# A longer annealed task order, and the last output rows in halves of columns, in an attention and gated-convolution kernel

## The chip, the cores and the metric

The kernel runs on one core of a Trainium2 chip. A core has a matrix engine (TensorE, "PE" in the profile; its weight loads are listed as "PEld"), a vector engine (VectorE, DVE), a scalar engine (ScalarE, ACT), a general engine (GpSimd, POOL) and a sync engine (SyncE, SP). The engines run side by side, each through its own list of instructions in order, and wait for each other through semaphores. Data come from device memory by DMA, issued here from the queues of SP (loads) and ACT (stores). The metric is the device time of one execution in microseconds.

## The reference

Inputs are queries, keys and values of 8 batches, 8 heads, 512 local and 32 global tokens, head size 64. A global token attends to all 544 tokens. A local token attends to the 32 global ones and to the local ones at a distance of at most 32. The attended rows (8 x 544 x 512) go through a gated block:

```
k_all, v_all = concat(global, local)
out_g = softmax(q_g k_all^T / 8) v_all
out_l = softmax(concat(q_l k_g^T, masked q_l k_l^T) / 8) v_all
x     = concat(out_g, out_l), heads side by side       # 8 x 544 x 512
gate  = sigmoid(sum over k of conv_w[k] * x shifted by k)   # 5 taps, causal
out   = (gate * (x @ w_val)) @ w_out                   # 512 x 512 weights
```

The weights come in float64, everything else in float32.

## The kernel before

**Units and batches.** The work is cut into 32 units, each two heads of one batch, so that one unit is 128 of the 512 columns of x for one batch; four units make a batch. The matmuls of the gated block are done in three passes of split operands (high times high, low times high, high times low), which stands for one float32 product.

**Tasks.** The kernel first adds some 1,400 named tasks to a `Plan`, each with an engine, a cost in ns, the tasks it depends on, and buffers it takes and gives. `ORDER` is one string, written out by hand, that names them in the order in which they are emitted. `Plan.order` walks it; every engine gets its own tasks in that order. Nothing is reordered later, so where a task's input is late, its engine stands with everything behind it. The costs of the plan set no order; they only decide how many idle matmuls `keep_clock` puts into expected gaps at the start.

**The names.** For unit u and head h:

- `s`u (PE, L478) scores into one PSUM tile per head (`sx`, `sy`); `mx`u.h (DVE, L490) mask and row minimum; `exp`u.h (ACT, L497); `t`u.h (PE, L503) transposes; `tc`u.h (ACT, L506) copies them to `pts`; `av`u (PE, L514) weighted values; `norm`u (DVE, L521 to L524) divides by the row sum; `xt`u (PE, L533) transposes; `xc`u (ACT, L537) copies.
- `halo`, `tap`, `conv`u.0 to .3 (DVE, L544 to L572): the five taps of the gate, one instruction each. For units 0 to 2 the taps are matmuls `pc`u.k (PE, L597) with diagonal weights that `dg`u (ACT, L586) builds. `sig`u (ACT, L605) is the sigmoid. `xh`u (ACT, L565) and `xl`u (DVE, L568) split x.
- For batch b: `gs`, `gmax`, `gexp`, `gt`, `gtc`, `gav`, `gnorm`, `gx`, `gxc` do the same for the global tokens.
- `g1.`b.e.t (PE, L621): first product, output block e, inner block t, three matmuls of 512 columns; `gv.`b.e (DVE, L629) multiplies by the gate; `gh.`b.e (ACT, L632) and `gl.`b.e (DVE, L635) split the result; `g2.`b.r.e (PE, L643): second product for 128 rows r; `ob.`b.r (ACT, L649) copies it out of PSUM; `st.`b.r (ACT's queue, L814) stores it. The PSUM tiles of g1 and g2 are two (`mm`), so a third waits until gv or ob has read the first.
- `w`k.s0 to .s7 (DVE, L282 to L294) turn a float64 weight block into two float32 parts, `w`k.high (ACT, L352) rounds the high part; k = 0 to 3 is w_val, 4 to 7 w_out.
- `iq`, `iv`, `wi` (SP, L314) issue the loads of a unit's queries and keys, of its values, and of a weight block. Each is made to wait for the PE task that precedes it in `ORDER`.

**Buffers.** One score tile per head (so `s`u+1 waits for `mx`u), two PSUM tiles for transposes, one for `av`, two for g1, g2 and `pc`; in SBUF four qk and four v tiles.

**The end.** Behind batch 7 come the 256 rows of all global tokens as a batch of their own, key `g`: `gxh`, `gxl`, `gconv` (DVE) build its x and gate, `sigg` its sigmoids, then g1, gv, gh, gl of 256 columns, and two g2 blocks of 128 rows. `ob.g.1` is the last copy: ACT takes columns 0 to 255 (L649), DVE columns 256 to 511 (L651). `st.g.r` stores four batches' rows by four DMAs of 32 rows, in turn from SP's and ACT's queues (L836).

**Table loads.** ACT loads another function table whenever it goes from exp to sigmoid or back (ACT_TABLE_LOAD in the profile).

Of the kernel before, what the change touches and what calls it, by code (L numbers as in the profile page):

```python
# [8 lines left out]
F32 = mybir.dt.float32  # L9
# [41 lines left out]
cw s0 mx0.0 mx0.1 w0.s0 exp0.1 exp0.0 w0.s1 w0.s2 s1 t0.1 mx1.0 t0.0 w0.s3 mx1.1 exp1.0 w0.s4 w0.s5 w0.s6 w0.high  # L51
tc0.1 tc0.0 av0 dg0 s2 exp1.1 norm0 mx2.0 xt0 xc0 w1.s0 t1.1 halo0 pc0.0 tc1.1 w1.s1 w1.s2 mx2.1 w1.s3 w0.s7 xh0 t1.0
w1.s4 exp2.1 tc1.0 exp2.0 pc0.1 w1.s5 pc0.2 xl0 av1 w1.s6 w1.high s3 norm1 mx3.0 dg1 exp3.0 t2.1 mx3.1 tc2.1 xt1 wi4
t2.0 w3.s0 w3.s1 w3.s2 pc0.3 tc2.0 t3.0 w3.s3 pc0.4 tc3.0 w1.s7 gs0 iq4 w3.s4 xc1 halo1 exp3.1 av2 w3.s5 w3.high
gmax0.0 wi5 pc1.0 gmax0.1 gexp0.0 iq5 norm2 w4.s0 xh1 pc1.1 w3.s6 w4.s1 w4.s2 gexp0.1 t3.1 xt2 w4.s3 tc3.1 w3.s7
conv0.3 gt0.0 s4 xc2 av3 pc1.2 w4.s4 gtc0.0 mx4.0 w4.high mx4.1 w4.s5 iq6 w5.s0 exp4.0 exp4.1 w4.s6 w5.s1 iq7 t4.0
w4.s7 w5.s2 gav0.0 tc4.0 gnorm0.0 t4.1 w5.s3 dg2 s5 tc4.1 w5.high gt0.1 pc1.3 w5.s4 gtc0.1 mx5.0 w2.s0 w5.s5 gav0.1
exp5.0 mx5.1 w5.s6 pc1.4 gnorm0.1 norm3 iv4 t5.0 exp5.1 w5.s7 tc5.0 t5.1 w2.s1 xl1 gx0 xt3 tc5.1 gxc0 gs1 wi6 halo2
iv5 xh2 fix0 iv6 conv1.3 gmax1.0 w2.s2 pc2.0 xc3 tap3 pc2.1 gmax1.1 fix1 w2.s3 pc2.2 gexp1.0 av4 xh3 pc2.3 pc2.4 norm4
iv7 w6.s0 halo3 w2.s4 xl2 gexp1.1 s6 w6.s1 w2.s5 gt1.0 conv2.3 wi7 w6.s2 xl3 mx6.0 gtc1.0 mx6.1 conv3.0 xt4 w6.s3  # L60
g1.0.0.0 g1.0.0.1 g1.0.0.2 w2.s6 w2.high w6.s4 conv3.1 exp6.0 g1.0.0.3 w6.s5 g1.0.1.0 g1.0.1.1 conv3.2 t6.0 g1.0.1.2
xc4 gav1.0 w6.s6 iq8 w6.high exp6.1 tc6.0 conv3.3 gnorm1.0 av5 g1.0.1.3 w6.s7 sig0 gt1.1 w2.s7 norm5 s7 gv.0.0 sig1
xt5 w7.s0 g1.0.2.0 gh.0.0 w7.s1 gtc1.1 gv.0.1 sig2 xh4 g1.0.2.1 sig3 mx7.0 tap4 g1.0.2.2 w7.s2 iq9 xc5 w7.s3 t6.1
g1.0.2.3 tc6.1 iq10 gl.0.0 g1.0.3.0 g1.0.3.1 av6 gav1.1 mx7.1 s8 gh.0.1 w7.s4 xl4 iq11 exp7.0 t7.0 gv.0.2 gl.0.1 w7.s5
g1.0.3.2 gnorm1.1 g1.0.3.3 iv9 gh.0.2 mx8.0 gl.0.2 iv8 exp7.1 gv.0.3 g2.0.0.0 gx1 exp8.0 g2.0.0.1 tc7.0 w7.s6 iv10
w7.s7 gh.0.3 gxc1 w7.high gl.0.3 mx8.1 g2.0.0.2 norm6 t7.1 exp8.1 t8.0 halo4 tc7.1 g2.0.0.3 g2.0.1.0 xh5 g2.0.1.1 t8.1
conv4.0 conv4.1 conv4.2 ob.0.0 halo5 g2.0.1.2 tc8.0 g2.0.1.3 tc8.1 conv4.3 xt6 xl5 gs2 tap5 xc6 gmax2.0 av7 xh6
conv5.0 g2.0.2.0 gmax2.1 norm7 conv5.1 g2.0.2.1 tap6 iv11 g2.0.2.2 ob.0.1 gexp2.0 gexp2.1 xl6 g2.0.2.3 conv5.2 xt7
gt2.0 conv5.3 s9 g2.0.3.0 halo6 st.0.0 g2.0.3.1 mx9.0 gtc2.0 conv6.0 xc7 g2.0.3.2 iq12 xh7 av8 mx9.1 gav2.0 iq13
exp9.0 exp9.1 s10 g2.0.3.3 xl7 ob.0.2 t9.0 norm8 gnorm2.0 conv6.1 st.0.2 st.0.1 conv6.2 tc9.0 t9.1 conv6.3 tc9.1 xt8  # L70
mx10.0 halo7 xc8 g1.1.0.0 gt2.1 gtc2.1 av9 mx10.1 tap7 gav2.1 exp10.1 conv7.0 g1.1.0.1 ob.0.3 conv7.1 g1.1.0.2
g1.1.0.3 s11 conv7.2 gnorm2.1 conv7.3 exp10.0 sig4 xh8 sig5 gx2 norm9 tap8 iv13 g1.1.1.0 t10.1 sig6 xl8 iq14 xt9 iv14
gv.1.0 g1.1.1.1 g1.1.1.2 gxc2 t10.0 halo8 tc10.1 gh.1.0 conv8.0 mx11.0 iq15 xc9 gl.1.0 g1.1.1.3 g1.1.2.0 sig7 halo9
g1.1.2.1 mx11.1 tap9 tc10.0 av10 st.0.3 g1.1.2.2 exp11.0 g1.1.2.3 conv8.1 s12 gv.1.1 gh.1.1 g1.1.3.0 conv8.2 gv.1.2
exp11.1 mx12.0 t11.0 g1.1.3.1 gh.1.2 exp12.0 t11.1 g1.1.3.2 iv12 gl.1.1 mx12.1 tc11.1 tc11.0 g1.1.3.3 norm10 gl.1.2
xh9 xl9 xt10 conv8.3 conv9.0 exp12.1 gv.1.3 g2.1.0.0 conv9.1 g2.1.0.1 t12.1 xc10 tc12.1 t12.0 tc12.0 av11 gh.1.3 gs3
g2.1.0.2 norm11 xt11 gl.1.3 xh10 gmax3.0 gmax3.1 g2.1.0.3 conv9.2 gexp3.0 g2.1.1.0 halo10 ob.1.0 gexp3.1 conv9.3
g2.1.1.1 tap10 xc11 g2.1.1.2 g2.1.1.3 ob.1.1 s13 iq16 xl10 xh11 av12 st.1.1 gt3.0 st.1.0 halo11 mx13.0 g2.1.2.0
conv10.0 mx13.1 g2.1.2.1 norm12 iv15 s14 exp13.0 exp13.1 conv10.1 conv10.2 mx14.0 conv10.3 xl11 iq17 gtc3.0 exp14.0
xt12 g2.1.2.2 t13.0 xc12 tap11 t13.1 g2.1.2.3 conv11.0 tc13.0 tap12 mx14.1 ob.1.2 tc13.1 g2.1.3.0 g2.1.3.1 av13  # L80
# [164 lines left out]
def attention_moe(ctx, tc, qk, vw, maskd, w_val, convT, w_out, out):  # L245
# [62 lines left out]
    def on_pe(ins):  # L308
        last_pe[:] = [ins.ins]
# [301 lines left out]
    def moe(key, n, x0, deps_x, deps_gate, before, store):  # L611
# [34 lines left out]
        def ob(r):  # L646
# [3 lines left out]
            if at < DM:  # L650
                V.tensor_copy(box["ob", r][:, at:], box["po", r][:, at:])  # L651
# [279 lines left out]
```

## Time and profile before

| | us |
|---|---|
| median of 3 runs | 372.37 |
| lowest, highest | 372.1, 372.75 |
| profiled execution, its own time | 372.69 |
| its span, first to last instruction | 370.9 |
| PE busy | 358.4 |
| DVE busy | 312.0 |
| ACT busy | 257.2 |
| mean granted TensorE clock | 0.999 |

The 1.8 us between the span and the profiled execution's own time lie around the instructions. A row of the page's groups reads: line, engine, operation, output <- inputs, shape, count | busy time, mean ns of one | idle time of the engine just before them and what ended it. A row of the timeline reads: start, duration, engine, line, operation. PE's matmuls are pipelined and overlap in the list, so the step from one start to the next says what one costs, and a busy PE isn't yet PE at its peak. In the last 40 us, DVE and ACT have little left to do, while PE runs through g1 and g2 of batch 7 and of the global tokens.

### The profile page before, as it was taken

The numbers are of one execution on the slowest core, as the hardware profiler recorded it, in microseconds if no ns is written. First come the engines' busy times: TensorE is split into PE (matmuls) and PEld (weight loads), VectorE is DVE, ScalarE is ACT, GpSimd is POOL, SyncE is SP. The second block draws the span as 40 slices with busy tenths as digits, with TensorE's granted clock in tenths as the row PEclk, the third lists the DMA queues.
The fourth block names the chain that finished last, engine by engine and source line by source line (L and its number), as shares of the span: only waits on it lengthen the run. The fifth ranks groups of instructions, "written<-read, shape, count | busy, mean of one in ns | idle before, by whom it ended". The sixth has DMA issues, their size and how long they took to land.

```text
span 370.9 us, 14811 instructions
## 1 busy us (share of the span) xinstructions
PE 358.4 (97%) x6347; PEld 280.5 (76%) x6347; DVE 312.0 (84%) x1094; ACT 257.2 (69%) x620; POOL 0.9 (0%) x7
## 2 busy tenths in 40 slices
PE   7899899999999999999999999999999999999995
PEld 3556557877878787787877887788788888888894
DVE  4899999999998897998689968999768877684861
ACT  3898867976798676976886668977876568434231
POOL 0000000000000000000000000000000000000000
PEclk9999999999999999999999999999999999999999
DMA  8995686495667174881339361975853010011112
GB/s 288 398 340 199 212 302 229 158 357 177 198 218 269 49 267 111 304 310 78 129 120 358 128 195 74 323 220 188 268 214 110 4 58 30 30 57 59 55 61 57
DMA packets 17250, 66.74 MB, mean 180 GB/s; under 512 B 1952, under 2 KB 4000, under 8 KB 17184
## 3 DMA queue, kind: packets, MB, share of 16 engines
q1 hardware_dynamic: 12240, 57.12, 44.4%
q10 hardware_dynamic: 4944, 8.67, 6.4%
q8 instruction: 50, 0.82, 0.9%
q14 instruction: 16, 0.13, 0.1%
HBM read 56.87 MB, written 8.91 MB: 177 GB/s over the span
## 4 chain that ended last, share of the span: by engine, by line
PE 81%; DVE 9%; DMA 7%; issue 1%; ACT 1%; ACTq 0%
PE po L643 23%; PE pv L621 23%; PE ax L514 8%; PE pt L503 6%; PE sx L478 5%; PE ax L533 3%; DMA wraw<-in_w_val_dram 3%; DMA v<-in_vw_dram 2%; PE sy L478 2%; PE ag L446 2%; DVE pm L490 2%; PE pvg L621 2%; PE pog L643 1%; PE gs_sx L403 1%; PE gpt L426 1%; PE pc L597 1%
## 5 line engine op out<-in xcount | busy, mean ns | idle before, releaser
L497 ACT ACTIVATE pm<-pm,mx 128x128 f32<-128x128 f32 x256 | 80.8, 394 | 13.9 <-DVE mx L490 13.4
L572 DVE SCALAR_TENSOR_TENSOR gate<-xc,cw,gate 128x512 f32<-128x512 f32 x116 | 86.1, 748 | 1.4
L643 PE MATMUL po<-woh,gh 128*128 128x512 f32 x128 | 54.2, 424 | 0.5 <-issue 0.5
L621 PE MATMUL pv<-xh,wvh 128*128 128x512 f32 x128 | 54.5, 426 | 0.0
L621 PE MATMUL pv<-xl,wvh 128*128 128x512 f32 x128 | 50.4, 394 | 0.0
L643 PE MATMUL po<-woh,gl 128*128 128x512 f32 x128 | 50.3, 393 | 0.0
L621 PE MATMUL pv<-xh,wvl 128*128 128x512 f32 x128 | 50.2, 392 | 0.0
L643 PE MATMUL po<-wol,gh 128*128 128x512 f32 x128 | 50.1, 391 | 0.0
L506 ACT COPY pts<-pt 128x512 f32<-128x512 f32 x64 | 36.6, 587 | 15.8 <-PE pt L503 15.3
L514 PEld LDWEIGHTS ax<-v,pts 128*32 128x32 f32 x2048 | 30.6, 109 | 11.2 <-issue 3.7
L503 PE MATMUL pt<-ident,pm 128*128 128x128 f32 x256 | 37.3, 274 | 1.3 <-DVE mx L521 0.6
L478 PE MATMUL sx<-qk 64*32 64x128 f32 x1024 | 38.0, 274 | 0.3 <-DVE mx L490 0.3
L503 PEld LDWEIGHTS pt<-ident,pm 128*128 128x128 f32 x256 | 30.5, 140 | 10.2 <-ACT pm L497 1.9
L478 PE MATMUL sy<-qk 64*32 64x128 f32 x1024 | 36.8, 274 | 0.5 <-DVE mx L490 0.4
L514 PE MATMUL ax<-v,pts 128*32 128x65 f32 x2048 | 35.7, 221 | 1.5 <-ACT pts L506 1.4
L478 PEld LDWEIGHTS sx<-qk 64*32 64x32 f32 x1024 | 28.7, 105 | 8.4 <-issue 3.6
L490 DVE CUSTOM_DVE_ANT_0 pm<-sx,mask 128x128 f32<-128x128 f32 x128 | 29.4, 286 | 4.1 <-PE sx L478 4.1
L632 ACT CAST gh<-gv 128x512 fp32r<-128x512 f32 x32 | 19.6, 622 | 18.2 <-DVE gv L629 15.9
L649 ACT COPY ob<-po 128x512 f32<-128x512 f32 x32 | 18.7, 584 | 18.5 <-PE po L643 18.4
L629 DVE TENSOR_TENSOR gv<-pv,gate 128x512 f32<-128x512 f32 x32 | 22.0, 687 | 10.8 <-PE pv L621 10.7
L537 ACT COPY xc<-ax 128x512 f32<-128x512 f32 x32 | 18.9, 589 | 15.4 <-DVE gate L572 12.9
L490 DVE CUSTOM_DVE_ANT_0 pm<-sy,mask 128x128 f32<-128x128 f32 x128 | 29.4, 286 | 0.0
(114 smaller groups left out, 653.4 us busy)
## 6 DMA issues: line engine op xcount, KB each, us to landing
v<-in_vw_dram SPq DMA_DIRECT2D x32, 975.0 KB, 6.7
qk<-in_qk_dram SPq DMA_DIRECT2D x32, 624.0 KB, 4.3
out_dram<-ob ACTq DMA_DIRECT2D x32, 256.0 KB, 2.4
wraw<-in_w_val_dram SPq DMA_DIRECT2D x4, 512.0 KB, 12.3
wraw<-in_w_out_dram SPq DMA_DIRECT2D x4, 512.0 KB, 4.6
mask<-in_mask_dram SPq DMA_DIRECT2D x1, 256.0 KB, 4.4
out_dram<-obg SPq DMA_DIRECT2D x4, 64.0 KB, 1.7
out_dram<-obg ACTq DMA_DIRECT2D x4, 64.0 KB, 2.0
```

Of the source, the lines that this page charges most:

```text
L478: on_pe(T.matmul((sx, sy)[h][32 * j:32 * j + 32, i, :], qkt[rows, 32 * m:32 * m + 32], qkt[rows, k0:k0 + P], start=True, stop=True))
L490: V.tensor_tensor_reduce(out=pm[:, h, i, :], in0=s[:, i, :], in1=mask[:, i, :], op0=ALU.add, op1=ALU.min, scale=-SCALE, scalar=3.0e38, acc ...
L497: A.activation(out=pm[:, h, i, :], in_=pm[:, h, i, :], func=AF.Exp, bias=mx[:, c:c + 1], scale=-1.0)
L503: on_pe(T.transpose(pt[:, i, :], pm[:, h, i, :], ident))
L506: A.copy(st[u]["pts"][:, h], st[u]["pt", h])
L514: on_pe(T.matmul(ax[32 * j:32 * j + 32, h, E1 * i:E1 * i + E1], pts[:, h, i, 32 * j:32 * j + 32], vt[:, block_win(4 * i + j), h, :], start ...
L537: A.copy(xc[:, KW - 1:], flat(u)[:, SL:])
L572: V.scalar_tensor_tensor(out=acc, in0=xc[:, k:k + SL], scalar=cw[:, u % NDT, k:k + 1], in1=acc, op0=ALU.mult, op1=ALU.add)
L621: on_pe(T.matmul(box["pv", e], w[:, e, t * P:t * P + P], x, start=(t == 0 and q == 0), stop=(t == NDT - 1 and q == 2)))
L629: V.tensor_tensor(out=box["gv", e], in0=box["pv", e], in1=gates[x0 + e], op=ALU.mult)
L632: A.copy(box["gh"][:, e, :], box["gv", e])
L643: on_pe(T.matmul(box["po", r], g[:, e, rs], w[:, e, :], start=(e == 0 and q == 0), stop=(e == NDT - 1 and q == 2)))
```

## The change

Two things change.

1. `ORDER` is replaced by another order of the same 1,435 tasks, with one new task, `half`. Dependencies, buffers and all instructions of those tasks but the last rows' are untouched. Its beginning, two stretches of its middle and its end, with the old ones:

```diff
-cw s0 mx0.0 mx0.1 w0.s0 exp0.1 exp0.0 w0.s1 w0.s2 s1 t0.1 mx1.0 t0.0 w0.s3 mx1.1 exp1.0 w0.s4 w0.s5 w0.s6 w0.high
-tc0.1 tc0.0 av0 dg0 s2 exp1.1 norm0 mx2.0 xt0 xc0 w1.s0 t1.1 halo0 pc0.0 tc1.1 w1.s1 w1.s2 mx2.1 w1.s3 w0.s7 xh0 t1.0
...
-xc4 gav1.0 w6.s6 iq8 w6.high exp6.1 tc6.0 conv3.3 gnorm1.0 av5 g1.0.1.3 w6.s7 sig0 gt1.1 w2.s7 norm5 s7 gv.0.0 sig1
-xt5 w7.s0 g1.0.2.0 gh.0.0 w7.s1 gtc1.1 gv.0.1 sig2 xh4 g1.0.2.1 sig3 mx7.0 tap4 g1.0.2.2 w7.s2 iq9 xc5 w7.s3 t6.1
...
-gl.g.2 gl.g.3 g2.g.0.1 g2.g.0.2 g2.g.0.3 g2.g.1.0 ob.g.0 g2.g.1.1 st.g.0 g2.g.1.2 g2.g.1.3 ob.g.1 st.g.1
+cw s0 dg0 mx0.0 mx0.1 w0.s0 exp0.0 w0.s1 exp0.1 w0.s2 s1 dg1 t0.1 tc0.1 t0.0 w0.s3 tc0.0 w0.s4 w0.s5 w0.s6 dg2 mx1.0
+mx1.1 av0 norm0 s2 exp1.1 mx2.0 exp1.0 xt0 w1.s0 xc0 halo0 w1.s1 exp2.0 w1.s2 mx2.1 t1.1 pc0.0 t1.0 tc1.1 xh0 tc1.0
...
+w5.s7 gav1.0 wi7 xh4 av5 w6.s3 gv.0.0 tc6.0 g1.0.2.0 gv.0.1 w6.s4 g1.0.2.1 norm5 sig2 gnorm1.0 mx6.1 sig3 w6.s5
+g1.0.2.2 g1.0.2.3 w7.s0 iq9 gh.0.0 xt5 w6.s6 gl.0.0 gh.0.1 gt1.1 w6.high g1.0.3.0 w7.s1 gl.0.1 g1.0.3.1 w7.s2 xc5
...
+gmax7.0 g1.5.0.1 conv25.0 g1.5.0.2 g1.5.0.3 gexp7.0 conv24.3 g1.5.1.0 g1.5.1.1 gmax7.1 xt26 g1.5.1.2 g1.5.1.3 gv.5.0
+gexp7.1 s28 xc26 av27 g1.5.2.0 g1.5.2.1 mx28.0 tap26 sig21 halo26 iv30 gt7.0 sig22 gh.5.0 conv25.1 exp28.0 iv29
...
+g2.g.0.3 st.7.2 g2.g.1.0 ob.g.0 st.g.0 g2.g.1.1 half g2.g.1.2 g2.g.1.3 ob.g.1 st.g.1
```

2. The last 128 rows (`g2.g.1`, `ob.g.1`, `st.g.1`). Its four PE tasks keep their names, but the first two now make columns 0 to 255 over all four inner blocks, the other two columns 256 to 511: 24 matmuls of 256 columns where there were 12 of 512. After the second, `half` copies the first 256 columns (ACT) and stores them from ACT's queue. `ob.g.1` then copies columns 256 to 383 on ACT and 384 to 511 on DVE, and each quarter is stored by one DMA, from ACT's and SP's queue. The stores of the global rows become one DMA for all four batches of a block, so `st.g.0` is one DMA from ACT's queue where it was four from two queues.

```diff
+            cols, es = slice(0, DM), [e]
+            if (key, r) == END:
+                cols, es = slice(e // 2 * HALF, e // 2 * HALF + HALF), [e % 2 * 2, e % 2 * 2 + 1]
+            for e in es:
+                for q, (g, w) in enumerate(((box["gh"], woh), (box["gh"], wol), (box["gl"], woh))):
+                    on_pe(T.matmul(box["po", r][:, cols], g[:, e, rs], w[:, e, cols], start=(e == 0 and q == 0),
+                             stop=(e == NDT - 1 and q == 2)))
...
         def ob(r):
+            if (key, r) != END:
+                box["ob", r] = sb.tile([P, DM], F32, tag="ob", name=f"ob{key}_{r}")
+                A.copy(box["ob", r], box["po", r])
+                return
+            at = HALF + HALF // 2
+            A.copy(box["ob", r][:, HALF:at], box["po", r][:, HALF:at])
+            V.tensor_copy(box["ob", r][:, at:], box["po", r][:, at:])
+
+        def first_half(r):
+
             box["ob", r] = sb.tile([P, DM], F32, tag="ob", name=f"ob{key}_{r}")
-            at = DM // 2 if (key, r) == ("g", n // P - 1) else DM
-            A.copy(box["ob", r][:, :at], box["po", r][:, :at])
-            if at < DM:
-                V.tensor_copy(box["ob", r][:, at:], box["po", r][:, at:])
+            A.copy(box["ob", r][:, :HALF], box["po", r][:, :HALF])
+            store(r, box["ob", r], ((A, 0, HALF),))
...
-    def store_g(r, o):
-        for s in range(P // SG):
-            (A if s % 2 else nc.sync).dma_start(out[r * (P // SG) + s, 0:SG, :], o[s * SG:s * SG + SG, :])
+    def store_g(r, o, parts):
+        n = P // SG
+        for queue, a, z in parts:
+            queue.dma_start(out[r * n:r * n + n, 0:SG, a:z], o[:, a:z])
```

`HALF` is 256, `END` is the block ("g", 1), and `parts` lists queue, first and last column of each store.

More of the change, by code (lines that the diff above doesn't have):

```diff
@@ L56 @@
[L56 to L60, printed above, removed]
@@ L66 @@
[L66 to L70, printed above, removed]
@@ L71 @@
[L71 to L80, printed above, removed]
```

155 lines of the change are left out of this document (88 added, 67 removed).

## The prediction

> **What bounds the kernel now.** I read the head of the page first, then a table by stage, then single rows where the stage is decided.
>
> ```profile
> PE 358.4 (97%) x6347; PEld 280.5 (76%) x6347; DVE 312.0 (84%) x1094; ACT 257.2 (69%) x620; POOL 0.9 (0%) x7
> 28.00:80.00 52.00, 49.22 (x995) 35.63 (x985) 50.78 (x191) 41.87 (x106) 0.00 (x0) 1.00 0.67 231
> 80.00:115.00 35.00, 34.57 (x749) 27.47 (x748) 32.92 (x115) 27.39 (x66) 0.00 (x0) 1.00 0.68 240
> 180.00:320.00 140.00, 139.58 (x2613) 112.44 (x2603) 115.51 (x414) 104.04 (x246) 0.00 (x0) 1.00 0.47 160
> ```
>
> The windows give the stretch, its length, then the busy time of PE, PEld, DVE and ACT. Over the whole span PE is the long line. From 28 to 80 us another engine sets the pace: DVE is busy 50.78 of 52.00 us and PE 49.22. From 180 to 320 us PE is busy 139.58 of 140 us, while DVE has 24 us to spare and ACT 36. So time can be won in three ways: PE gets more done for the same DVE work early, PE loses fewer waits later, or the tail behind the last matmul shrinks. An order moves work but removes none.
>
> **The early stage, counted.** The new order runs the same tasks, so I compared the sets of tasks ahead of two places. In the old order, 66 PE tasks and 99 DVE tasks stand up to the point where `g1.0.2.0` follows `gv.0.0`, which frees its bank. In the new order the next place that DVE decides is `g2.0.0.2`, which needs `gl.0.2`. Up to there it has the same 66 and 99 tasks, without exception, and 14 PE tasks and 16 DVE tasks more. The 16 are gv.0.1 to 0.3, gl.0.0 to 0.2, mx7.0, mx7.1 and the eight steps of w7.
>
> ```profile
> 57.89 0.69 DVE L286 SCALAR_TENSOR_TENSOR wa<-wraw,wa 128x512 int32<-128x512 int32 x1
> 58.50 0.42 DVE L288 TENSOR_SCALAR wraw<-wa 128x512 int32<-128x512 int32 x1
> 58.83 0.42 DVE L293 TENSOR_SCALAR wraw<-wraw 128x512 int32<-128x512 int32 x1
> ...
> 64.92 0.68 DVE L629 TENSOR_TENSOR gv<-pv,gate 128x512 f32<-128x512 f32 x1
> 65.52 0.42 DVE L282 TENSOR_SCALAR wa<-wraw 128x512 int32<-128x512 int32 x1
> ...
> 66.91 0.28 DVE L490 CUSTOM_DVE_ANT_0 pm<-sx,mask 128x128 f32<-128x128 f32 x1
> ...
> 67.75 0.48 DVE L560 TENSOR_SCALAR gate<-xc,cw 128x512 f32<-128x512 f32 x1
> ```
>
> These timeline rows are DVE without a gap, so the step from one start to the next is the price of a task: gv 0.60 (64.92 to 65.52), two-input weight step 0.61 (57.89 to 58.50), one-input step 0.33 (58.50 to 58.83), mx 0.84 (66.91 to 67.75). A weight is three steps of the first kind and five of the second, 3.5 us (I take 3.6); I price gl like gv, same form. Sum: 6 x 0.60 + 2 x 0.84 + 3.6 = 8.9 us. DVE left gv.0.0 at 65.52, so it leaves gl.0.2 at 74.4. With about 0.15 us for the end of the instruction and the hand-over, PE can start `g2.0.0.2` at **74.55**.
>
> ```profile
> 73.37 0.66 PE L503 MATMUL pt<-ident,pm 128*128 128x128 f32 x4
> 73.78 0.48 PE L621 MATMUL pv<-xh,wvh 128*128 128x512 f32 x1
> ...
> 76.75 0.40 PE L643 MATMUL po<-woh,gh 128*128 128x512 f32 x1
> ```
>
> In the old order the row at 76.75 is the same `g2.0.0.2`. By then PE has done the same tasks and two more, t7.0 (73.37 to 73.78, 0.41 us) and the single matmul of gx1. Same content: 76.3. **The new order is ahead by 76.3 - 74.55 = 1.75 us.** The condition is that the common 99 tasks still end at 65.5. Bounds: between 28 and 80 us DVE idles 1.2 us. If that went, the gain would be near 3; if it came twice, near 0.5. I take it unchanged, since buffers and first loads are the same and two moves work against each other there: dg0 and dg1 now stand ahead of exp0 and tc0 on ACT (about 1.5 us each), while w0.high and exp1.0 step back behind them.
>
> SP's order moves too, and here it costs.
>
> ```profile
> 54.49 0.33 SPq L314 DMA_DIRECT2D wraw<-in_w_out_dram  x1
> 62.09 0.15 DVE L452 TENSOR_SCALAR gd<-ag 128x1 f32<-128x1 f32 x1
> wraw<-in_w_out_dram SPq DMA_DIRECT2D x4, 512.0 KB, 4.6
> ```
>
> The load of w7 waits on SP for the PE task ahead of it in the line: that was gt1.0 (issued at 54.49, needed by w7.s0 at 65.52), and is now gav1.0, with iq8 ahead of it. In the old run gav1.0 ended just before gnorm1.0's first row at 62.09. In the new one it may end between 60 and 62, as it too waits for a load (v7, the DMA piece of the old chain there); plus 4.6 the data land between 64.7 and 66.7. From w7.s0 to gl.0.2 the new order has 9.2 us of DVE tasks (w7 3.6, three gl and two gv 3.0, mx7 1.7, two steps of w6 0.9), so w7.s0 is due at 74.4 - 9.2, about 65.2. So DVE waits between nothing and 1.4 us in its full stretch; I take 0.5. **Early stage: -1.75 + 0.5, about -1.2.**
>
> **Later stage.** The gain survives only if PE is not held again.
>
> ```profile
> PE po L643 <- issue: 0.5, 1, 0.5
> PE ag L446 <- issue: 0.4, 1, 0.4
> PE ax L514 <- ACT pts L506: 0.4, 1, 0.4
> PE gxt L458 <- DVE xg L454: 0.3, 1, 0.3
> 176.01 0.91 PE ax L514 x64
> 309.36 1.05 PE ax L514 x64
> ```
>
> That is PE's list of waits from 80 to 320 us, and two pieces of the chain: 1.6 us in four places. I leave them as they are, neither removed nor added. Counting neighbours in the two orders, PE changes between the three kinds of matmul (scores, weighted values, the rest) 122 times for 124, and meets dearer neighbours less often. A change costs about 0.1 us where I can see one (the 64 matmuls of an av take 1.05 at 309.36, behind a g1, and 0.91 at 176.01, behind a gav of their own kind): between -0.2 and -0.6, and I take **-0.3**.
>
> ACT pays for this order. Sigmoids are now split between exps.
>
> ```profile
> L605 ACT ACT_TABLE_LOAD x7 | 9.0, 1283 | 0.1
> 60.90 1.28 ACT L605 ACT_TABLE_LOAD   x1
> 62.20 1.15 ACT L605 ACTIVATE gate<-gate 128x512 f32<-128x512 f32 x2
> ```
>
> Along ACT's line the old order goes between exp and sigmoid 13 times, the new one 23 times: 10 x 1.283 = 12.8 us more (mean of the first row), all in batches 3 to 6. What hides them is ACT's 36 us of idle time between 180 and 320 us, so I cost them at nothing. Uncovered, each is 1.28 us on PE's line. The cover is thinnest where gexp7, exp28 and exp29 alternate with sig20 to sig23: four added loads (5.1 us) over 27 PE tasks of some 19 us, where ACT's usual quarter of idle time is 4.9 us.
>
> The Trainium skill (page "ScalarE: Activation LUTs", section "What ACT_TABLE_LOAD costs") gives 1283 ns and a drain of about 1380 ns more for each switch, and advises batching by set. The trace agrees with the load alone: it ends at 62.18 and the sigmoid starts at 62.20, so no drain shows behind it. By the page a switch is 2.66 us, ten are 26.6 us of ACT, and rival 4 below would decide from the first exposed one.
>
> **The tail.**
>
> ```profile
> 366.37 0.39 PE L643 MATMUL pog<-woh,glg 128*128 128x512 f32 x1
> 366.79 0.37 ACT L649 COPY obg<-pog 128x256 f32<-128x256 f32 x1 [2.13 <-PE pog L643]
> 367.20 0.42 DVE L651 COPY obg<-pog 128x256 f32<-128x256 f32 x1 [4.53 <-ACT obg L649]
> 367.65 0.85 ACTq L836 DMA_DIRECT2D out_dram<-obg  x2
> 361.30 5.46 PE pog L643 x24
> L437 ACT COPY pgt<-gpt 128x128 f32<-128x128 f32 x16 | 4.4, 273 | 0.0
> 357.02 0.28 PE L621 MATMUL pvg<-xgl,wvh 128*128 128x256 f32 x1
> 357.14 0.28 PE L621 MATMUL pvg<-xgh,wvl 128*128 128x256 f32 x1
> out_dram<-ob ACTq DMA_DIRECT2D x32, 256.0 KB, 2.4
> out_dram<-obg ACTq DMA_DIRECT2D x4, 64.0 KB, 2.0
> ```
>
> Matmuls: 12 of 512 columns become 24 of 256. These step 0.115 us (357.02 to 357.14, with a new weight load each), so 24 x 0.115 = 2.76 against 12 x 0.227 = 2.73 (5.46 / 24 in the chain): no cost. Behind the last one, ACT copies 128 columns (0.27, L437) for 256 (0.37), DVE 128 for 256 (0.42; less 128 columns at about 0.1 us per 100, 0.29), and the last matmul, with half the columns, ends about 0.1 sooner: -0.33. Each queue issues one store and not two: half of 0.85, -0.42. The pieces get four times as many and a quarter as long; landing lies between 2.0 and 2.4 by the two store rows, +0.1. Alone that is -0.65.
>
> But DVE's copy here waited 4.53 us, for ACT's copy, though the two touch different columns; PE had ended before. So accesses of two engines to one such tile are put in a row, whole tile by whole tile. The new `half` reads columns 0 to 255 of the bank into which PE must go on writing. If it is treated alike, PE stands from its 12th small matmul until ACT's copy is through: 0.32 to the copy's start (366.37 to 366.79, less 0.1), 0.37, 0.04 on, less one step of 0.115: 0.6, perhaps 0.4 as PE's starts are stamped early. I take +0.5, between 0 and 0.65. **Tail: -0.65 + 0.5 = about -0.1.**
>
> The Trainium skill ("PSUM — Partial Sum Buffer", section "PSUM bank collisions raise a hardware error") speaks against this part: two engines may not touch one bank in the same partitions at once, even in different columns, and software must guard by bank. The row of the DVE copy agrees with it. By that rule the wait is sure and the tail is -0.1; without it, -0.65.
>
> **Sum.** -1.2 - 0.3 - 0.1 = -1.6 us. The profiled run took 372.69 with a span of 370.9, so span 369.3 and 371.1 in all; against the median of 372.37: **370.8 us**. A measurement of this kernel tells 0.2% (0.75 us) from no change.
>
> **Rivals.**
> 1. *The forecast* (0.45): 369.8 to 371.6.
> 2. *Later waits go too* (0.21): the 1.6 us above fall, perhaps the 0.5 of the half as well: 370.8 - 2.1 = 368.7. For it: from 180 us DVE and ACT have room to run ahead. Against: these waits are short and scattered, and a new order makes its own.
> 3. *The gain is eaten between 80 and 115 us* (0.19). DVE is busy 32.92 of 35 there; being ahead, PE leans on DVE more. If DVE's 2.1 us of idle time stay, PE waits what it won: only -0.4 remains, 372.0.
> 4. *Slower* (0.15): table loads come out on PE's line in the stretch of sig20 to sig23. Each exposed load is 1.28 us; one leaves 372.1, two give 373.4, all four added there 375.9. It decides from the second.
> 5. *The half does not do what it says*: PE's wait takes back what the tail saves. That is the sum's own -0.1, and at the bounds of the wait the tail is between -0.65 and 0; it changes no case's sign.
>
> The range takes the forecast, most of 2 and all of 3: 368.2 to 372.8. Faster by over 0.2% (cases 1 and 2) 0.66, within it (3) 0.19, slower (4) 0.15.
>
> **What would show it.** The early step: `g2.0.0.2` (third group of po) near 75 and DVE over 97% busy from 28 to 75 us; worse than taken if DVE waits over 0.5 us for the w7 load. PE's changes: the windows from 180 us keep PE at 10 of 10. ACT: 22 or 23 table loads beside the start's, and no PE wait on exp, pts or gh longer than 0.5 in batches 3 to 6; a row of that kind over 1 us is case 4. Tail: a hole of about 0.5 us among the pog matmuls ended by ACT's copy, then about 3.9 us from the last matmul's start to the end where it was 4.5. If the first gain is missing, the common 99 tasks did not end at 65.5.

## The result and the profile after

| | median, us | range | runs | ratio to before (95%) |
|---|---|---|---|---|
| before | 372.59 | 371.81 to 372.96 | 14 | |
| after | 374.46 | 373.36 to 376.86 | 14 | 1.0057 (1.0041 to 1.0073) |

The changed kernel is **slower by 0.57%** (the medians differ by 1.9 us), where 1.6 us of gain were forecast. 374.46 lies outside the forecast range of 368.2 to 372.8. The profiled execution of after took 376.86 us (span 375.1), the longest of its fourteen, so its trace shows more loss than the median does. The runs of after spread over 3.5 us, those of before over 1.2.

The head of the page and the three windows of before, now from after (columns as above: stretch, length, busy PE, PEld, DVE, ACT):

```profile
PE 360.5 (96%) x6358; PEld 281.1 (75%) x6358; DVE 311.1 (83%) x1094; ACT 269.4 (72%) x631; POOL 0.8 (0%) x7
```
```profile
28.00:80.00 52.00, 50.69 (x1014) 36.09 (x998) 50.86 (x192) 40.16 (x100) 0.00 (x0) 1.00 0.64 220
80.00:115.00 35.00, 34.31 (x747) 26.71 (x746) 33.20 (x119) 27.27 (x66) 0.00 (x0) 1.00 0.67 237
180.00:320.00 140.00, 138.62 (x2430) 111.24 (x2419) 113.62 (x401) 112.03 (x247) 0.00 (x0) 1.00 0.46 157
```

DVE is as full as before in the first stretch (50.86 for 50.78), and PE is busy 1.5 us longer there. From 180 to 320 us PE is 1.0 us *less* busy than before (138.62 for 139.58), which was not forecast. ACT has 12.2 us more work.

To find where the time goes I compared the start of the same PE task in both traces. The tasks ahead of the first row differ by t7.0 and one small matmul, 0.41 us; the others are comparable as they stand.

| start of | before | after | after minus before |
|---|---|---|---|
| `g2.0.0.2` (batch 0) | 76.75 | 75.03 | -1.72 |
| `g1.7.0.0` (batch 7) | 333.43 | 333.28 | -0.15 |
| `g2.g.1.0` (last block) | 363.87 | 364.09 | +0.22 |
| last matmul | 366.37 | 367.98 | +1.61 |
| end of the span | 370.89 | 375.06 | +4.17 |

So an early gain arrives, is given back on the way in this execution, and the last 11 us lose 4 us. The end, as the timeline of after shows it (start, duration, engine, line, operation, and in brackets the idle time ahead of it and its releaser):

```profile
364.09 0.28 PE L649 MATMUL pog<-woh,ghg 128*128 128x256 f32 x1
...
364.29 0.59 ACT L655 COPY obg<-pog 128x512 f32<-128x512 f32 x1 [1.88 <-PE pog L649]
...
364.90 1.14 ACTq L855 DMA_DIRECT2D out_dram<-obg  x1
...
365.40 0.28 PE L649 MATMUL pog<-woh,glg 128*128 128x256 f32 x1
...
366.14 0.37 ACT L664 COPY obg<-pog 128x256 f32<-128x256 f32 x1 [1.27 <-PE pog L649]
...
366.57 0.39 PE L649 MATMUL pog<-woh,ghg 128*128 128x256 f32 x1 [0.89 <-ACT obg L664]
...
367.98 0.28 PE L649 MATMUL pog<-woh,glg 128*128 128x256 f32 x1
...
368.30 0.27 ACT L658 COPY obg<-pog 128x128 f32<-128x128 f32 x1 [1.78 <-PE pog L649]
368.59 0.55 ACTq L855 DMA_DIRECT2D out_dram<-obg  x1
368.60 0.29 DVE L659 COPY obg<-pog 128x128 f32<-128x128 f32 x1 [5.73 <-ACT obg L658]
368.91 0.71 SPq L855 DMA_DIRECT2D out_dram<-obg  x1
```

Two things are to be seen. First, PE stands from 365.40 to 366.57 in the last block, for the copy of `half` (L664). That copy could have begun soon after 365.40, but ACT was still issuing the store of the block before, an issue of **1.14 us** (364.90 to 366.04). Second, the last copy is through at 368.89 and the last store is issued by 369.62, yet the span ends at 375.06. What is left there is landing. In numbers: PE's part of the last block, from `g2.g.1.0` to the start of the last matmul, is 3.89 us for 2.50 (+1.39), and the tail behind it 7.08 for 4.53 (+2.55).

The waits of PE from 180 to 320 us in after (what waited for what: total, times, longest) show the other loss:

```profile
PE ag L448 <- DMA v<-in_vw_dram: 1.2, 2, 0.8
PE gxt L460 <- DVE xg L456: 0.2, 1, 0.2
```

`gav5.0` and `gav7.0` wait for the data of v. That row is absent in before, whose list for this window has one row, 0.4 us of another kind.

### The profile page after: what moved, and what is told of

It reads as the page before. It is cut to its first block, busy times and chain, and to the rows that moved or that the text cites. A ratio compares the mean times of both kernels' runs of the same rounds, so it can differ in the third digit from the quotient of the medians.

```text
span 375.1 us, 14840 instructions
## 1 busy us (share of the span) xinstructions
PE 360.5 (96%) x6358; PEld 281.1 (75%) x6358; DVE 311.1 (83%) x1094; ACT 269.4 (72%) x631; POOL 0.8 (0%) x7
## 4 chain that ended last, share of the span: by engine, by line
PE 69%; DVE 14%; DMA 11%; ACT 3%; issue 1%; ACTq 0%
PE pv L623 19%; PE po L649 18%; DMA v<-in_vw_dram 8%; PE ax L516 7%; PE pt L505 6%; PE sx L480 4%; PE ax L535 3%; DVE pm L492 2%; PE ag L448 2%; DVE gateg L714 2%; PE sy L480 2%; DMA out_dram<-ob 2%; PE pvg L623 1%; DMA craw<-in_convT_dram 1%; PE gpt L428 1%; PE pog L649 1%
## 5 line engine op out<-in xcount | busy, mean ns | idle before, releaser
L623 PEld LDWEIGHTS pv<-xh,wvh 128*128 128x128 f32 x128 | 24.1, 188 | 7.3 <-issue 1.9
```

The lines of the kernel that those rows point to most:

```text
L623: on_pe(T.matmul(box["pv", e], w[:, e, t * P:t * P + P], x, start=(t == 0 and q == 0), stop=(t == NDT - 1 and q == 2)))
```

## The experiments

All ratios are to the kernel before. "Ending" is the last block (`g2.g.1`, `half`, `ob.g.1`) and the two stores of the global rows.

### The order alone, the ending alone

**a_order** is before with the new `ORDER`, without `half`, and with the old ending. **b_tail** is after with the old order up to the last block.

```diff
 # a_order: before.py
-<old ORDER>
+<new ORDER, "half" left out>
 # b_tail: after.py
-<new ORDER>
+<old ORDER up to ob.g.0> st.g.0 g2.g.1.1 half g2.g.1.2 g2.g.1.3 ob.g.1 st.g.1
```

> New order without the task half; last rows copied and stored as in the kernel before. Theory T (the loss sits in the last rows: PE standing for the half's copy, and stores that land late; the order itself is about even): in the two traces PE starts g2.g.1.0 at 363.87 (before) and 364.09 (after), so +0.2 us, ratio 1.000 to 1.001, and the tail from the last matmul's start to the end is 4.5 us as before. Rival O (the order lost it): ratio 1.004 or more.

> Old order up to the last block, then the change's own ending with half and its stores. Theory T: PE's part of the last block takes 3.9 us where it took 2.5 (+1.4), the tail behind it is 4.5 to 7 us, so +1.4 to +2.5 us, ratio 1.004 to 1.007, and single runs spread by 2 us or more. Rival O: ratio 1.000 to 1.001.

| | median, us | range | runs | ratio (95%) |
|---|---|---|---|---|
| a_order | 370.54 | 369.52 to 372.5 | 12 | 0.9948 (0.9931 to 0.9965) |
| b_tail | 376.42 | 375.98 to 376.69 | 5 | 1.0100 (1.0086 to 1.0114) |

Against 372.71 us for before in the same set of runs, the order alone gains 2.2 us and the ending alone costs 3.7. Their sum, +1.5, is close to the +1.9 of both together. **The ending is the whole loss, and the order gains, as it was forecast to.** Both runs went past what was expected of them, which was no change for a_order (1.000 to 1.001) and 1.004 to 1.007 for b_tail, with a spread of 2 us or more. b_tail's five runs lie within 0.7 us, so the spread of after doesn't come from the ending. In b_tail's profile the last block on PE and the tail take 3.89 and 7.09 us, as in after.

The table loads can be ruled out by a_order too, as it has all of them: its two lines of loads read (line, engine, operation, count | busy, mean ns | idle before)

```profile
L605 ACT ACT_TABLE_LOAD x12 | 15.4, 1283 | 0.2
...
L497 ACT ACT_TABLE_LOAD x9 | 11.5, 1283 | 0.1
```

Before, the line of the sigmoid (L605) had seven loads and that of the exponentials (L497) five. So 9 of the 10 added ones stand in these rows (the tenth is in the line of the global tokens' exponentials, L419), and in a_order's list of PE's waits from 180 to 320 us no row names ACT:

```profile
PE ag L446 <- DMA v<-in_vw_dram: 1.8, 2, 0.9
PE gxt L458 <- DVE xg L454: 0.2, 1, 0.2
```

### The landing: one store of four rows

The prediction put the landing of the new stores between those of two other kinds of store. The records of the DMA packets say otherwise. Each store of the ending comes with some small packets of 4 bytes, which I take for one per share into which it was cut. By queue and size, in the ending (counted from the packet records of the traces; us from the span's start):

```
kernel     stores of the ending             data packets               4-byte packets   tail
before     8: [32 rows x 512 columns] each  256 of 2048 B              128 = 8 x 16     4.53
after      4: [4 x 32 rows x columns] each  128 of 2048 B 366.20-370.89  16 = 4 x 4     7.08
                                            128 of 1024 B 370.06-372.25
                                            256 of  512 B 371.42-373.77
h_store    2: [4 x 32 rows x 512 columns]   256 of 2048 B 366.23-374.47   8 = 2 x 4     9.27
d_qmajor   4: [16 x 8 rows x columns]       128 of 2048 B 369.50-370.79  64 = 4 x 16    4.03
f_banks   12: [32 rows x columns] each      128 of 2048 B, 256 of 1024  192 = 12 x 16   3.88
```

Where the store's outer dimension is 4 (four batches), it ends in four small packets, where it is 32 or 16, in sixteen. The share of the 16 DMA engines that is busy fits: in these rows of the DMA view each digit is the busy share of a slice in tenths, first before from 365 to 371 us, then after from 366 to 374.

```profile
DMA  0004997899810000000000088997991000000000
```
```profile
DMA  0342070101222122222222222222222222221110
```

Before, two short bursts at 8 or 9 tenths; after, one long stretch at 2 tenths. A store of four outer rows keeps about a quarter of the engines busy. The packet records agree: in the ending of after mostly four or five packets are under way at one time and never more than seven, in that of d_qmajor often 14 to 17. The packets themselves are hardly slower, 134 ns in the mean for 2048 bytes against 124 in d_qmajor. The stores of after then queue one behind the other: the half's packets start when those of `st.g.0` are nearly out (370.06), though it was issued at 366.55.

The Trainium skill states the rule (page "DMA: Bandwidth & Descriptors", section "Why a DMA increments its semaphore by 16 and not by 1"): the number of DMA engines is the largest one up to 16 that divides the slowest dimension (sizes of 1 left out) of both sides of the copy, and each engine taking part posts one completion. The small packets, 4 and 16, agree with it. The prediction did not weigh it, and it spoke against this change.

Three runs test it. **h_store** puts the merged store, and nothing else of the change, into before. **d_qmajor** keeps after whole, its four stores too, but lays the global rows out token by token, so that a store has 16 outer rows of 8 batches. **c_perbatch** splits the stores of after by batch again, most of them issued from SP.

```diff
 # h_store: before.py
-        for s in range(P // SG):
-            (A if s % 2 else nc.sync).dma_start(out[r * (P // SG) + s, 0:SG, :], o[s * SG:s * SG + SG, :])
+        n = P // SG
+        A.dma_start(out[r * n:r * n + n, 0:SG, :], o)
 # d_qmajor: after.py
-        hv, lv, acc = (h[NU + dt].rearrange("p (b q) -> p b q", b=B) for h in (xs_h, xs_l, gates))
+        hv, lv, acc = (h[NU + dt].rearrange("p (q b) -> p b q", b=B) for h in (xs_h, xs_l, gates))
...
-        n = P // SG
+        n = P // B
...
-            queue.dma_start(out[r * n:r * n + n, 0:SG, a:z], o[:, a:z])
+            queue.dma_start(out[:, r * n:r * n + n, a:z].rearrange("b q c -> q b c"), o[:, a:z])
 # c_perbatch: after.py
-            queue.dma_start(out[r * n:r * n + n, 0:SG, a:z], o[:, a:z])
+            for s in range(n):
+                queue.dma_start(out[r * n + s, 0:SG, a:z], o[s * SG:s * SG + SG, a:z])
...
-            store(r, box["ob", r], ((A, 0, HALF),))
+            store(r, box["ob", r], ((nc.sync, 0, HALF),))
...
-            parts = ((A, HALF, HALF + HALF // 2), (nc.sync, HALF + HALF // 2, DM)) if (key, r) == END else ((A, 0, DM),)
+            parts = ((A, HALF, HALF + HALF // 2), (nc.sync, HALF + HALF // 2, DM)) if (key, r) == END else ((nc.sync if key == "g" else A, 0, DM),)
```

> The kernel before with one thing changed: each of the two stores of global rows is one DMA of 128 rows from ACT's queue. No half, no new order. Theory S: 4 small packets per store, the issue takes 1.1 us, the second store's packets start behind the first one's, tail 7 to 8 us where it was 4.5: 375 to 376.4, ratio 1.007 to 1.010. Rival (large merged stores are harmless, the 512 B pieces were the trouble): one issue fewer per queue, 372.3 to 372.7, ratio 0.999 to 1.000.

> The changed kernel, but the global block's rows lie token by token (8 batches inside a token) so that one store of 128 rows has 16 outer rows and not 4; same number of DMAs, same bytes, same queues, same 512 B and 1 KB pieces. Theory S (four DMA engines): 16 small packets at the end of each store, landing near 2 us, tail about 3.9 us, 373.2 to 373.8 and a spread under 1 us. Rival (small pieces): no change against the kernel after, 374.5 with its spread. The vector work on the global block now strides; if that costs, gconv gets longer than 2.4 us.

> The changed kernel, but every store of the global rows cut into one DMA per batch of 32 rows (as before the change), those of st.g.0 and of the half from SP's queue and no longer from ACT's. Theory S (the merged DMA is what lands late: in the trace of after each of them ends with 4 small packets where one of before ends with 16, so it runs on four of the 16 DMA engines): landing back near 2 us, four issues of 0.4 us on the last queue, tail 5 us, ACT free for the half's copy 0.7 us sooner, so 373.0 to 373.6 and a spread under 1 us. Rival (landing is late because the pieces are small, 512 B): tail stays over 5.5 us in the profile and the runs keep their spread.

| | median, us | range | runs | ratio (95%) | last block on PE | tail |
|---|---|---|---|---|---|---|
| before | | | | | 2.50 | 4.53 |
| after | 374.46 | 373.36 to 376.86 | 14 | 1.0057 (1.0041 to 1.0073) | 3.89 | 7.08 |
| h_store | 376.67 | 376.37 to 377.75 | 4 | 1.0111 (1.0097 to 1.0125) | as before | 9.27 |
| d_qmajor | 377.32 | 376.7 to 378.48 | 4 | 1.0130 (1.0112 to 1.0149) | 3.47 | 4.03 |
| c_perbatch | 372.61 | 371.83 to 374.8 | 10 | 1.0006 (0.9991 to 1.0021) | 3.47 | 5.81 |

*h_store* is 1.1% slower than before: with eight stores turned into two, both from ACT's queue, and nothing else changed, the tail goes from 4.53 to 9.27 us, more than the 7 to 8 expected. All its packets have 2048 bytes, as in before, so the loss doesn't need the small pieces of after. The issues changed too (first before, then h_store: minimum, median and maximum ns of an issue, first and last start):

```profile
L836 SPq DMA_DIRECT2D out_dram<-obg x4: 315/385/414, 364.7 to 368.0; - x4
L836 ACTq DMA_DIRECT2D out_dram<-obg x4: 375/410/441, 364.7 to 368.1; - x4
```
```profile
L836 ACTq DMA_DIRECT2D out_dram<-obg x2: 552/851/1150, 364.9 to 367.9; - x2
```

A merged store takes 1.15 us of the issuing engine at first and 0.55 the second time.

*d_qmajor* is the counter-test of the landing and a failure as a kernel. Its four stores have the bytes, the sizes of pieces, the queues and the order of after's; the outer dimension goes from 4 to 16, and with it the order in which the rows lie. The 128 packets of the first store are out in 1.29 us for 4.69, and the tail is 4.03 us for 7.08, so that **3.05 us of the tail hang on the outer dimension**. The DMA engines from 369 to 375 us:

```profile
DMA  0005996799458972000000001762870000000000
```

But the layout makes DVE go through the parts and the gate of the global rows with a stride, and that costs more ahead of the ending than it saves there (373.2 to 373.8 us were expected). The rows of the gate and of the low part (count | busy, mean ns), first after, then d_qmajor:

```profile
L714 DVE SCALAR_TENSOR_TENSOR gateg<-xgT,cw,gateg 128x256 f32<-128x256 f32 x16 | 7.8, 485 | 0.6
...
L709 DVE TENSOR_TENSOR xgl<-xgT,xgh 128x256 fp32r<-128x256 f32 x4 | 1.7, 417 | 0.0
```
```profile
L714 DVE SCALAR_TENSOR_TENSOR gateg<-xgT,cw,gateg 128x256 f32<-128x256 f32 x16 | 11.5, 719 | 0.6
...
L709 DVE TENSOR_TENSOR xgl<-xgT,xgh 128x256 fp32r<-128x256 f32 x4 | 2.7, 672 | 0.0
```

That is 5.2 us more work for DVE (with 0.5 us of L712). DVE has no room for it: though little was said to be left for it in the last 40 us, in before it is busy 9.9 of the 10.5 us from 345 to 355.5. So PE waits at the start of the last batch:

```profile
PE pvg L623 <- DVE xgl L709: 4.7, 1, 4.7
```

*c_perbatch* is 1.9 us below after by the medians and level with before; its last block and tail together take 9.28 us for 10.97. 373.0 to 373.6 were expected. Its tail of 5.81 us is still above the 4.53 of the old ending, and its runs spread over 3 us: a tail over 5.5 with the spread kept had been named as the sign of the rival, that small pieces land late. d_qmajor speaks against that rival, as it has the same pieces and a tail of 4.03. What is long in c_perbatch is SP's row of issues: SP has twelve stores to issue, at 0.31 to 0.44 us each, and its last one starts at 368.24, 2.5 us behind the end of DVE's copy (365.46 + 0.29). Between its eighth and ninth store SP stands for 1.1 us (365.82 to 366.94); its list of waits names the landing of an earlier store for that, but no run tests it.

### PE's wait inside the last block

In c_perbatch ACT has no merged store to issue, and PE's part of the last block is 3.47 us; after has 3.89. The row behind the wait in c_perbatch:

```profile
363.43 0.39 PE L649 MATMUL pog<-woh,ghg 128*128 128x256 f32 x1 [0.46 <-ACT obg L664]
```

So of the 1.14 us by which PE stands in after (3.89 less 23 steps of 0.12 between the 24 small matmuls), **0.72 is the wait for the copy, and 0.42 ACT's long issue ahead of that copy**. Two runs take away the reason for the wait: columns 256 to 511 go to a PSUM tile of their own, so that no engine reads the tile into which PE writes. **g_bank** does only this. **f_banks** also leaves DVE alone with the second half and issues one store per batch, in turn from SP and ACT.

```diff
 # g_bank and f_banks: after.py
+                box["pb", r] = None
+            if (key, r) == END and e == 2:
+                box["pb", r] = ps.tile([P, HALF], F32, tag="pt", name=f"pb{key}_{r}", bufs=2)
...
+                    dst = box["po", r][:, cols] if box["pb", r] is None else box["pb", r]
-                    on_pe(T.matmul(box["po", r][:, cols], g[:, e, rs], w[:, e, cols], start=(e == 0 and q == 0),
+                    on_pe(T.matmul(dst, g[:, e, rs], w[:, e, cols], start=(e == 0 and q == 0),
...
 # g_bank only
-            A.copy(box["ob", r][:, HALF:at], box["po", r][:, HALF:at])
-            V.tensor_copy(box["ob", r][:, at:], box["po", r][:, at:])
+            A.copy(box["ob", r][:, HALF:at], box["pb", r][:, :at - HALF])
+            V.tensor_copy(box["ob", r][:, at:], box["pb", r][:, at - HALF:])
 # f_banks only
-            A.copy(box["ob", r][:, HALF:at], box["po", r][:, HALF:at])
-            V.tensor_copy(box["ob", r][:, at:], box["po", r][:, at:])
+            V.tensor_copy(box["ob", r][:, HALF:], box["pb", r])
...
-            parts = ((A, HALF, HALF + HALF // 2), (nc.sync, HALF + HALF // 2, DM)) if (key, r) == END else ((A, 0, DM),)
+            parts = ((A, HALF, DM),) if (key, r) == END else ((A, 0, DM),)
...
-            queue.dma_start(out[r * n:r * n + n, 0:SG, a:z], o[:, a:z])
+            for s in range(n):
+                (queue if s % 2 else nc.sync).dma_start(out[r * n + s, 0:SG, a:z], o[s * SG:s * SG + SG, a:z])
```

> The changed kernel, only with columns 256 to 511 of the last block in a PSUM tile of their own; its stores stay (one DMA per part, four outer rows). Theory S (the end is set by the queue of packets on four DMA engines): PE's last matmul comes 1.2 us sooner than in after (2.7 us behind g2.g.1.0 where it took 3.9), but the tail grows by about as much, to 7.5 us or more, and the time stays within 0.7 us of after's 374.5. Rival B (the wait for the bank is what was lost): 373.2 or less.

> The new order with half; columns 256 to 511 of the last block go to a PSUM tile of their own, DVE alone copies them, and each store of global rows is again four DMAs of 32 rows in turn from SP and ACT. Theory T: no wait of PE behind the half's copy (2.6 us from g2.g.1.0 to the last matmul's start), tail 4.0 us where it was 4.5, so 0.3 to 0.4 us under a_order: 370.1 to 370.3, ratio 0.993 to 0.995, up to 1 us more spread for the loads of values. Rival (splitting the last rows costs in itself, whatever the bank and the stores): 371 or more.

| | median, us | range | runs | ratio (95%) | last matmul starts | tail |
|---|---|---|---|---|---|---|
| g_bank | 374.06 | 373.75 to 374.78 | 4 | 1.0038 (1.0025 to 1.0051) | 364.65 | 8.33 |
| f_banks | 369.65 | 369.16 to 371.02 | 6 | 0.9927 (0.9910 to 0.9943) | 364.07 | 3.88 |

g_bank wins 1.1 us on PE and gives it back behind it: the last matmul starts 8.33 us ahead of the end, the longest tail of any version of after. The first store's packets alone run from 364.02 to 368.75 us, and the others queue behind them. **With the merged stores the end is set by the DMA queue, not by PE**, and a wait removed on PE is worth little: 374.06 lies inside the runs of after.

f_banks has neither loss (370.1 to 370.3 us were expected). Its timeline shows ACT's copy of the first half (363.08) beside matmuls that go on in steps of 0.12, and DVE's copy straight behind the last one:

```profile
362.63 0.28 PE L653 MATMUL pog<-woh,glg 128*128 128x256 f32 x1
...
362.75 0.28 PE L653 MATMUL pbg<-woh,ghg 128*128 128x256 f32 x1
...
364.07 0.28 PE L653 MATMUL pbg<-woh,glg 128*128 128x256 f32 x1
```
```profile
363.08 0.37 ACT L667 COPY obg<-pog 128x256 f32<-128x256 f32 x1 [0.98 <-PE pog L653]
...
364.38 0.42 DVE L662 COPY obg<-pbg 128x256 f32<-128x256 f32 x1 [4.29 <-DMA out_dram<-obg]
```

The last row names a store as what ended DVE's wait, but DVE starts 0.31 us behind the start of the last matmul, as ACT's copy does in c_perbatch (364.85 to 365.17), so the matmul is the likelier releaser. PE's part is 2.75 us, the 23 steps of 0.12 without a wait, and the tail 3.88. Together 6.63 us, for 7.03 in before and 10.97 in after.

### The waits for v

The other loss shows in the profiles of after and of a_order, but not in that of c_perbatch, which has the same order: so it comes in some executions only. In a_order's profile PE takes 289.10 us from `g2.0.0.2` to `g2.g.1.0`, in that of c_perbatch 286.89: some 2 us. That fits the spread (a_order: nine runs between 369.52 and 370.89, three between 372.33 and 372.5, of which one was profiled), but with one profile for each kernel it isn't shown for the other runs. In after's timeline SP issues the loads of v for `gav5.0` and its neighbour from 193.20, two of them within 3.8 us, and PE reaches `gav5.0` at 204.62:

```profile
193.20 3.79 SPq L316 DMA_DIRECT2D v<-in_vw_dram  x2
```
```profile
204.62 0.29 PE L448 MATMUL ag<-v,pgt 96*32 96x65 f32 x6
205.69 0.55 PE L448 MATMUL ag<-v,pgt 96*32 96x65 f32 x6 [0.78 <-DMA v<-in_vw_dram]
```
```profile
v<-in_vw_dram SPq DMA_DIRECT2D x32, 975.0 KB, 7.2
```

The load's median time to landing is 7.2 us (6.7 in before), and the second one here was issued at 196.66, some 8 us before its use. In c_perbatch the loads are issued at the same distance and land in time, so the late issue leaves no room, and the landing time decides. **e_iv** is a_order with four load issues moved ahead in `ORDER`: `iv22` and `iv23` behind `av19`, `iv30` behind `av26`, `iv29` behind `av27`. **i_best** puts these moves into f_banks, and **j_gxl** also moves `gxl3` ahead of `gconv0`, since in several profiles PE stood 0.38 us between `g1.g.0.3` and `g1.g.1.0`.

```diff
 # e_iv: a_order, i_best: f_banks
-xc18 av19 g1.3.0.3 gmax5.0
+xc18 av19 iv22 iv23 g1.3.0.3 gmax5.0
...
-iv28 xh25 av26 gs7
+iv28 xh25 av26 iv30 gs7
...
-s28 xc26 av27 g1.5.2.0
+s28 xc26 av27 iv29 g1.5.2.0
... (and the four taken out at their old places)
 # j_gxl: i_best
-gconv1 gconv0 gxl3 g1.g.0.0
+gconv1 gxl3 gconv0 g1.g.0.0
```

> The new order with the old ending (as a_order), and four loads of values issued sooner: iv22 and iv23 right behind av19, iv30 right behind av26, iv29 right behind av27. Theory V (the new order issues these loads so late that two gav tasks wait for them in many executions; in the profile of a_order 1.16 us at gav5.0 and 1.18 us at gav7.0, none in that of c_perbatch): those waits go, 369.4 to 369.9 where a_order had 370.5, ratio 0.991 to 0.993, and the runs spread over 1 us and no longer over 3. Rival (loads land late because the memory is slow at these moments, not because they are issued late): waits stay, ratio 0.995 with the same spread.

> The two repairs together: the last block's second half of columns in a PSUM tile of its own with one store per batch (f_banks, 369.65 us) and the four loads of v moved behind later weighted values (e_iv, 369.75 us). Theory (the last block's wait and the waits for v are separate losses, so they add): f_banks has 0.65 us less behind the start of its last matmul than e_iv (3.88 against 4.53), and e_iv's fastest run is 369.36, so about 369.0 us with a spread below 1 us, and no wait of the matmuls for v between 180 and 320 us. Rival (f_banks had already escaped the waits for v in its fast runs, so the moved loads give nothing): 369.6 us, the same as f_banks.

> The same with gxl3 moved ahead of gconv0 in the order, so that the low part of the global rows' last input block is ready one gate earlier. Theory (the 0.38 us between g1.g.0.3 and g1.g.1.0 is a wait for gxl3 alone): the stall goes, 0.3 to 0.4 us less than i_best, about 368.6 us. Rival (gconv0 then comes 0.4 us later and sigg, gv.g.0 with it, so the wait goes to the first block that needs gv.g.0): the same as i_best.

| | median, us | range | runs | ratio (95%) |
|---|---|---|---|---|
| a_order | 370.54 | 369.52 to 372.5 | 12 | 0.9948 (0.9931 to 0.9965) |
| e_iv | 369.75 | 369.36 to 370.27 | 4 | 0.9921 (0.9908 to 0.9934) |
| f_banks | 369.65 | 369.16 to 371.02 | 6 | 0.9927 (0.9910 to 0.9943) |
| i_best | 369.86 | 369.61 to 370.01 | 5 | 0.9923 (0.9912 to 0.9935) |
| j_gxl | 369.58 | 368.75 to 372.21 | 6 | 0.9924 (0.9897 to 0.9951) |

In the profile of e_iv the waits for v are gone: PE's list from 180 to 320 us has one row left, and PE is busy 139.74 us of that window (138.62 in after, 139.58 in before). Its four runs spread over 0.9 us, for 3.0 in a_order.

```profile
PE gxt L373 <- DVE xg L369: 0.2, 1, 0.2
```
```profile
180.00:320.00 140.00, 139.74 (x2456) 112.31 (x2458) 114.58 (x397) 113.19 (x249) 0.00 (x0) 1.00 0.45 157
```

`g1.7.0.0` starts at 330.66 there, 2.8 us ahead of before, where in a_order's profile it started at 332.73. The moves were not tried one by one.

i_best missed: 369.0 us were expected if the two repairs add, and it came out at 369.86, level with f_banks. The pieces are there in its profile (no wait for v from 180 to 320 us, PE's last part 2.75, tail 3.88), and its runs spread over 0.4 us only. But the ending with halves is worth no more than 7.03 - 6.63 = 0.4 us over the old one of e_iv, and the runs don't resolve that. f_banks seems to have escaped the waits in most of its runs. j_gxl does remove its stall (the step from `g1.g.0.3` to `g1.g.1.0` is 0.36 us, 0.72 in i_best), yet its median is 0.3 us from i_best with runs from 368.75 to 372.21: not told apart. The run of 372.21 has the moved loads too, so they don't keep every execution from being long; what made that one long is open. i_best is the version to keep: all its five runs are at 370.01 us or less, and the lowest of before is 371.81. But e_iv, with the old ending, is as fast. What is shown to gain is the order with the moved loads; that the halves of columns gain anything isn't shown.

## Why the prediction was wrong

**The early stage: the count right, one term by luck.** `g2.0.0.2` was forecast at 74.55 with DVE never waiting, or near 75 with the late load. It started at 75.03, and from 28 to 75 us DVE was busy 46.00 of 47.00 us, 97.9%, for "over 97%":

```profile
65.08 0.69 DVE L296 SCALAR_TENSOR_TENSOR wraw<-wraw 128x512 f32<-128x512 int32 x1
65.69 0.42 DVE L284 TENSOR_SCALAR wa<-wraw 128x512 int32<-128x512 int32 x1
...
75.03 0.50 PE L649 MATMUL po<-woh,gh 128*128 128x512 f32 x1
```
```profile
28.00:75.00 47.00, 45.69 (x988) 31.90 (x971) 46.00 (x166) 36.63 (x90) 0.00 (x0) 1.00 0.64 221
```

But the half microsecond didn't come from the load of w7. `w7.s0` was due at about 65.2 and ran at 65.69, one ordinary step of 0.61 behind the row ahead of it, so DVE didn't wait there. In a_order, which has the same order, `w7.s0` runs at 65.15 without a wait and `g2.0.0.2` at 74.41, which is the sum without the term; after is half a microsecond behind a_order already at `w1.s0` (17.37 for 16.87). Counting the tasks of the engine that sets the pace, up to a common place of both orders, held to 0.15 us in a_order. That +0.5 came out in after as well was luck.

**The order as a whole: right in direction, larger in size.** -1.2 and -0.3 make -1.5; a_order measured 2.2 us less than before by medians (0.9948, 0.9931 to 0.9965). Rival 3, the gain eaten between 80 and 115 us, fell with it. In some executions it is partly given back, to loads of v that come late. The prediction weighed SP's order for w7 only; that each of the 32 loads of v is issued at a place that `ORDER` sets was in its description and not in its sum. Rival 2 (the later waits go too) is what e_iv comes near to: its waits of PE from 80 to 320 us are 0.4 us for 1.6 in before, and its median is 3.0 us below before, where the rival had 3.7.

**Rival 4, exposed table loads: fell.** The ten loads are there (+12.2 us of ACT), and no row of PE's list of waits between 180 and 320 us names ACT. The forecast of a slower kernel stood on the wrong mechanism.

**PE's wait for `half`: the mechanism right, the size too small.** +0.5 was taken, 0.65 the upper bound. PE stood for 1.14. The wait itself is 0.72 (c_perbatch, d_qmajor) and gone with a tile of its own (f_banks), as expected of a wait for the whole tile. The other 0.42 is ACT, which was still issuing `st.g.0`: 1.14 us where the working took a store issue at about 0.4. The 24 small matmuls, priced at 0.115 each and so at no cost, stepped by 0.12, which makes them 0.15 us longer than 12 steps of 0.227.

**The landing: the step that failed.** The working said "landing lies between 2.0 and 2.4 by the two store rows, +0.1" and "Each queue issues one store and not two", which made the tail 3.9 us. The rows used were stores of 32 or 128 outer rows, and the new one has 4. The tail was 7.08 us; with 16 outer rows and all else of the ending unchanged it was 4.03, so the rest of that sum held to 0.15 us. Without the +0.1 the sum is 4.53 - 0.33 - 0.42 = 3.78, so the term measured 3.3 us, and 3.05 of it went with the outer dimension. (The pieces weren't "four times as many and a quarter as long" either: 128 packets of 2048 bytes became 128 of 1024 and 256 of 512. d_qmajor has the same pieces and no such loss.) No store with so small an outer dimension occurred in the trace of before, and its price was given bounds from two rows that are not its neighbours.

**The sum.** The order gave -2.2 for the -1.5 forecast (a_order), the ending +3.7 for -0.1 (b_tail).

## What to carry to other kernels

- Before several stores are merged into one, read the outermost dimension of the new one: a store over 4 batches ran on about a quarter of the DMA engines, and its extra landing cost more than the issues it saved. At the end of a kernel, where nothing hides it, keep one store per batch and spread them over two queues.
- To copy half of a result out while the matrix engine fills the other half, give the halves separate PSUM tiles, and see that the engine which copies isn't busy issuing a store.
- Where a task order also places the loads, check each load's issue against its use with the landing time of the profile (7 us here, with 8 us of room it was late in some runs); a spread over runs that came with the order was the sign of it here.

## What the runs showed of the hardware that was not expected

- A store with an outer dimension of 4 ended in 4 small packets of 4 bytes, one of 16 or 32 in 16, and 256 KB took 4.69 us of packets for 1.29 (after and d_qmajor), with mostly four or five packets under way at one time in the ending of after, and often 14 to 17 in that of d_qmajor.
- The issue of such a store held ACT for 1.14 us the first time and 0.55 the next, for 0.34 to 0.45 of a store per batch; with 16 outer rows the first took 0.64.
- One strided layout of 128x256 operands raised DVE's two-input instruction from 485 to 719 ns and the subtraction from 417 to 672 (after and d_qmajor).
